# A recurrent-attention kernel gets a table of PE places, late values spread over the steps, 32-column values, one softmax product per unit and a held store queue

## The chip, the cores and the metric

The kernel runs on one core of one Trainium2 chip. The metric is device time in microseconds (us) of one launch. "Before" is timed by the median of five runs: 1677.59 us (1676.94 to 1679.9). The profile is one further execution, taken by the hardware profiler. Engine names: PE is TensorE's matmul, PEld its weight load, DVE VectorE, ACT ScalarE, POOL GpSimd, SP SyncE, which here only issues DMAs.

## What is computed

Two layers, each a memory-augmented recurrent attention (A) and a dense relu layer (B), both with a layer norm in front and a residual; x is 2048 x 512 in bf16. The weights are the same in both layers.

```python
def A(x, mem0, Wq, Wk, Wv, Wo):          # M = 8 memory rows, 64 segments of 32 rows, 32 heads of 128
    mem = mem0
    for s in range(n_seg):
        h = concat([mem, x[:, 32*s:32*(s+1)]])            # 40 rows
        q, k, v = h @ Wq, h @ Wk, h @ Wv                  # per head
        scores = q @ k.T * Dh ** (-0.5)                   # masked: causal, memory rows see all
        o = softmax(scores) @ v @ Wo
        mem = o[:, :M]                                    # the next segment's memory
        outs.append(o[:, M:])
x = x + A(layernorm(x), ...)
x = x + relu(layernorm(x) @ w1) @ w2
x = x + A(layernorm(x), ...)
x = x + relu(layernorm(x) @ w1) @ w2
```

A segment needs the memory rows of the one before: within a layer the segments run in a chain.

## The kernel before

**Steps.** A step k handles segment k of layer 0 and segment k - 4 of layer 1 (`DELTA = 4`) side by side. There are 68 steps: 0 to 3 have layer 0 alone (40 columns in the attention matmuls), 4 to 63 both (80 columns), 64 to 67 layer 1 alone. In a step:

- `values` (L772): h times Wv in four parts of 8 matmuls of 512 columns. Each matmul's stationary operand is 64 columns wide, so two run side by side in 64-column tiles of the array. The result is copied from the PSUM bank (`fill`) to `vw`. `place_values` moves layer 0's rows of it into `V0` by DMA (L809).
- The 32 heads go in five `UNITS`: three of eight heads (0 to 2), two of four (3 and 4). For each unit `queries_keys` (L819; matmul L832) computes q and k of four heads in 16 matmuls each, copied from PSUM by ACT or DVE (`copy_on`, L724 on ACT, L726 on DVE). `scores` (L844) multiplies them (L861), and the softmax follows on DVE and ACT: `block` (mask, L872), `top` (L876), `sub` (L879), `exp` on ACT (L883), `total` (L886), `recip` (L889), `mul` (L909). The product P is transposed on PE (`turn`, by `across`, L519), copied to `PT` (`keep`), and multiplied with V in `attend` (L947), whose result is copied to `OT`.
- `project` (L974) multiplies OT with Wo, all units into one bank `st`. Its result goes two ways: by DVE into `HT` of the next step (L990, the memory rows, the recurrence), and by `rows` into `OX`. Both read the one bank.

After every second step `finish_pair` transposes OX back (`turn`), adds the residual and runs `dense_layer` and `layernorm` for the 64 rows of each layer.

**Late values.** Layer 0's own rows are known from the start. For the first 16 of each segment's 32 rows the values are computed ahead, 16 groups of four segments (`late_values`, L752, four parts each), and stored in DRAM (`vh`). `place_values` fetches them into `V0` (L802) for each step. Groups 1 to 4 (`EARLY`) use w1's and w2's room before these weights are loaded; later ones use `vg`.

**Order.** Nothing is left to a scheduler at build time: a class `Plan` collects operations with an engine, an assumed cost, what they read and write and a buffer, orders all of them and emits them in that order, so that each engine's queue is fixed. In before it schedules forward and backward three times (`PASSES`), with one assumed latency per engine (`LAT`), one priority offset per kind of operation (`AHEAD`), and four numbers (`RULE`: how far ahead it looks, what staying in a tile mode is worth, and when an operation marked `spare` is put off or fills a gap). `spare` are the late values. Operations of tile `EITHER` run in whole tiles or in 64-column tiles, whichever PE is in. `copy_op` and the products may go to either of two engines, by whichever ends first.

**Weights.** `load_weights` (L381) issues eight DMAs of 2 MB on POOL in the order v0, v2, q0, k0, q2, k2, o0, o2. The plan assumes a landing time for each (`available`); the stores of `vh` and the loads on SP are ordered after an assumed time `loaded`, but wait for nothing. `prepare` (L461) sets buffers to zero on DVE or POOL.

The softmax product of a large unit goes in two halves, each on POOL or DVE; of a small one in one:

```python
        for b0, b1 in ((0, 1), (1, 2)) if nx == 2 else ((0, 2),):
...
            plan.op((POOL, DVE), (t_pool(2 * na * L), t_dve(2 * na * L)), mul, r=[es, sm],
                    w=[("P", p, b, x) for b in range(b0, b1) for x in xs])
```

Of the kernel before, what the change touches and what calls it, by code (L numbers as in the profile page):

```python
# [20 lines left out]

PE, ACT, DVE, POOL, SP = range(5)
LAT = (0.26, 0.16, 0.16, 0.20, 1.70)

WHOLE, COL64, EITHER = range(3)
TURN = 0.11
PASSES = 3

RULE = (0.052, 0.937, 39.167, 24.322)
AHEAD = {
    "attend.ev": -1.96, "attend.mm": -0.95, "dense_layer.mm": -0.85, "dense_layer.relu": 5.2, "finish_pair.add": -5.1,
    "finish_pair.add0": 0.5, "finish_pair.add1": -6.36, "finish_pair.turn": 2.26, "finish_pair.widen": 0.01,
    "late_values.cp": -9.2, "late_values.put": 0.92, "layernorm.aggr": -7.15, "layernorm.keep": 0.04,
    "layernorm.norm": -2.92, "layernorm.power": -0.26, "layernorm.stats": 2.48, "layernorm.turn": -30.25,
    "load_dense.dma1": -1.13, "load_dense.dma2": -2.4, "load_group.get": -0.77, "load_weights.dma": -0.55,
    "make_ident": 4.63, "make_mask": 7, "place_values.dma": 17.27, "prep_x.cp": -1.81, "prepare.get_memory": -2.96,
    "prepare.get_x": -8.86, "prepare.keep": -0.84, "prepare.place": 0.28, "prepare.zero": -0.64,
    "prepare.zero_banks": -5.82, "prepare.zero_columns": -5.11, "prepare_group.load": -0.14,  # L40
    "prepare_group.put": -0.18, "project.ev": 10.38, "project.first": 0.18, "project.mm": -0.98,
    "project.rows": -4.33, "queries_keys.ev": 4.81, "queries_keys.mm": 0.09, "scores.block": 0.96,
    "scores.exp": -1.91, "scores.keep": -25.3, "scores.mm": 0.21, "scores.mul": -8.63, "scores.recip": -1.72,
    "scores.sub": -9.57, "scores.top": 1.48, "scores.total": 48.55, "scores.turn": 1.1, "values.mm*": -36.32,
}

LOAD, BESIDE = 5.5, 0.4

EARLY = 4


def t_act(n):
    return 0.09 + 0.833e-3 * n


def t_dve(n, rate=1):
    return 0.085 + 1.042e-3 * n / rate
# [5 lines left out]

class Pool:


    def __init__(self, tiles, ordered=False):
        self.tiles, self.ordered, self.asked = tiles, ordered, 0

    def reset(self):  # L70
        self.free, self.taken = [(0.0, i, None) for i in range(len(self.tiles))], 0
# [7 lines left out]
    def when(self, bufs):  # L79
        if len(self.free) < len(bufs) or self.ordered and bufs[0].no != self.taken:  # L80
            return 1e9
        return sorted(f[:2] for f in self.free)[len(bufs) - 1][0]

    def take(self, b):
        f = min(self.free, key=lambda f: f[:2])
        self.free.remove(f)
        self.taken += 1
        b.i = f[1]
        return f[2]
# [12 lines left out]
class Op:  # L102
    __slots__ = ("eng", "cost", "fn", "preds", "succs", "bufs", "new", "given", "ready", "start", "end", "wait",
                 "after", "seq", "tile", "lag", "mode", "more", "both", "spare")


class Plan:
    def __init__(self):
        self.ops, self.writer, self.readers = [], {}, {}
        self.given = {}  # L110
# [4 lines left out]
    def op(self, eng, cost, fn, r=(), w=(), tile=WHOLE, lag=None, more=0.0, spare=False):  # L115
        o = Op()
        o.both = dict(zip(eng, cost)) if isinstance(eng, tuple) else None
        if o.both:
            eng, cost = eng[0], cost[0]
        o.eng, o.cost, o.fn, o.succs, o.seq, o.tile = eng, cost, fn, [], len(self.ops), tile  # L120
        o.mode, o.more, o.spare = tile, more, spare
        o.lag = LAT[eng] if lag is None else lag
# [26 lines left out]
    def forward(self, prio):  # L149

        look, stay, far, room = RULE
        for pool in self.pools:
            pool.reset()
        for b in self.bufs:
            b.left, b.end = len(b.users), 0.0  # L160
        for o in self.ops:
            o.wait, o.ready, o.after = len(o.preds), o.given, []
        free = [0.0] * 5
        cand = [[] for _ in range(5)]
        for o in self.ops:
            if not o.wait:
                for e in o.both or (o.eng,):
                    cand[e].append(o)
        count, tile = 0, WHOLE
        while count < len(self.ops):  # L170
            best = None
            for e in range(5):
                lo, starts = None, []
                for o in cand[e]:
                    t = max(o.ready, free[e])
                    if o.both and any(max(o.ready, free[i]) + c < t + o.both[e] for i, c in o.both.items() if i != e):
                        continue
                    for pool, bufs in o.new:
                        t = max(t, pool.when(bufs))
                    starts.append((t, o))  # L180
                    if lo is None or t < lo:
                        lo = t
                if lo is not None and lo < 1e9 and (best is None or lo < best[0]):
                    best = (lo, e, starts)
            assert best is not None, "no operation can be planned"
            lo, e, starts = best
            def rank(c):
                return (prio[c[1].seq] - (stay if e == PE and c[1].tile in (tile, EITHER) else 0.0), c[1].seq)

            t, o = min((c for c in starts if c[0] <= lo + look), key=rank)  # L190
            if e == PE and o.spare:

                soon = [c for c in starts if t < c[0] < t + o.cost and prio[c[1].seq] < prio[o.seq] - far]
                if soon:
                    due = min(c[0] for c in soon)
                    t, o = min((c for c in starts if c[0] + room * c[1].cost * c[1].spare <= due and c[0] <= due), key=rank)
            o.start = t
            for i in o.both or ():
                if i != e:
                    cand[i].remove(o)  # L200
            if o.both:
                o.eng, o.cost, o.lag = e, o.both[e], LAT[e]
            cand[e].remove(o)
            for pool, bufs in o.new:
                for b in bufs:
                    last = pool.take(b)
                    if last is not None:
                        o.after += last.users
            o.end = o.start + o.cost
            if e == PE:  # L210
                o.mode = tile if o.tile == EITHER else o.tile
                if o.mode != tile:
                    o.end, tile = o.end + TURN, o.tile
                if o.mode == COL64:
                    o.end += o.more
# [869 lines left out]
```

## Time and profile before

| what | value |
|---|---|
| median of five runs | 1677.59 us |
| the profiled execution | 1679.95 us, span 1678.2 us |
| mean granted TensorE clock | 0.994 |
| matmuls of queries and keys (L832) | 17,408: 15,360 of 80 columns, 2,048 of 40 |
| matmuls of the projection (L974) | 8,704: 7,680 of 80 columns, 1,024 of 40 |
| value matmuls in 64-column tiles (L780) | 2,688: 2,176 of the steps, 512 late ones |
| softmax products (L909) | 270 on DVE, 274 on POOL |
| HBM traffic | 33.89 MB read, 12.45 MB written |

The span is the time from the first to the last instruction; launch and end lie around it. Busy time of PE holds pipelined matmuls whose ends are modelled: the mean of a matmul's row (200 ns for L832) is its time in the pipe, not its pace. The pace is read from the starts of successive groups in the timeline. In a row "work<-HT,Wq_sb" is out<-in by the kernel's tile names; a wait is written as the waiting row, then "<-" and what released it.

### The profile page before, as it was taken

What the parts mean: (1) busy time and instruction counts of PE and PEld (TensorE: products, weight loads), DVE (VectorE), ACT (ScalarE), POOL (GpSimd) and SP (SyncE); (2) the same over time, 40 slices, a digit from 0 to 9 for tenths busy, and PEclk for the clock granted to TensorE, in tenths of its full rate; (3) what the DMA queues carried; (4) which work ended last, traced back from release to release, by engine and by line L of the source; (5) the groups of instructions that cost most, each with busy time, mean ns of one, the idle gap of its engine ahead of it and who ended that gap; (6) DMA issues with size and microseconds to landing.
All of it is one profiled execution on the core that took longest, in us unless ns stands there. A gap on an engine that the chain in (4) does not pass through costs nothing.

```text
span 1678.2 us, 90465 instructions
## 1 busy us (share of the span) xinstructions
PE 1627.0 (97%) x40568; PEld 1395.8 (83%) x40568; DVE 1066.5 (64%) x3090; ACT 1062.7 (63%) x2679; POOL 246.1 (15%) x603
## 2 busy tenths in 40 slices
PE   6899999999999999999999999999999999999998
PEld 3678888888888888888888888888888888888886
DVE  5457566666676575667666665676566656766655
ACT  3466666666666666666666666666666666666664
POOL 3111111111111111111111111111111111111100
PEclk9899999999999999999999999999999999999999
DMA  9711111111110101000000000101010000000000
GB/s 369 238 49 35 38 38 27 35 41 33 32 39 18 37 18 31 22 21 24 19 24 21 20 22 18 27 18 25 19 27 16 19 23 21 18 18 19 18 5 7
DMA packets 32503, 64.88 MB, mean 39 GB/s; under 512 B 7049, under 2 KB 16913, under 8 KB 32113
## 3 DMA queue, kind: packets, MB, share of 16 engines
q1 hardware_dynamic: 25984, 39.38, 8.6%
q0 software_dynamic: 4608, 18.19, 2.9%
q8 instruction: 318, 5.21, 1.3%
q10 hardware_dynamic: 1520, 1.52, 0.3%
q14 instruction: 73, 0.59, 0.1%
HBM read 33.89 MB, written 12.45 MB: 28 GB/s over the span
## 4 chain that ended last, share of the span: by engine, by line
PE 79%; DVE 13%; DMA 4%; issue 1%; ACT 1%; POOL 1%; SPq 0%; POOLq 0%; DVEq 0%; ACTq 0%
PE work L832 32%; PE fill L780 16%; PE st L974 13%; PE fill L519 8%; PE work L947 3%; PE work L861 3%; DMA Wo_sb<-in_A_Wo_dram 3%; PE work L519 2%; DVE OT L726 2%; DVE sm L886 2%; DMA V<-vw 2%; DVE PT L726 1%; DVE ln L528 1%; DVE xg L616 1%; POOL P L909 1%
## 5 line engine op out<-in xcount | busy, mean ns | idle before, releaser
L832 PE MATMUL work<-HT,Wq_sb 128*128 128x80 bf16 (+1 forms) x8704 | 391.0, 200 | 7.5 <-DVE HT L990 6.7
L832 PE MATMUL work<-HT,Wk_sb 128*128 128x80 bf16 (+1 forms) x8704 | 390.2, 199 | 6.9 <-DMA Wk_sb<-in_A_Wk_dram 4.5
L974 PE MATMUL st<-OT,Wo_sb 128*128 128x80 bf16 (+1 forms) x8704 | 354.3, 200 | 2.5 <-DMA Wo_sb<-in_A_Wo_dram 2.3
L832 PEld LDWEIGHTS <-Wq_sb 128*128 128x128 bf16 x8704 | 333.0, 99 | 26.7 <-issue 9.5
L832 PEld LDWEIGHTS <-Wk_sb 128*128 128x128 bf16 x8704 | 336.5, 100 | 8.5 <-DMA Wk_sb<-in_A_Wk_dram 5.4
L974 PEld LDWEIGHTS <-Wo_sb 128*128 128x128 bf16 x8704 | 322.3, 100 | 23.1 <-issue 17.8
L872 DVE TENSOR_TENSOR es<-work,maskb 128x320 f32<-128x320 f32 (+2 forms) x340 | 137.4, 404 | 304.7 <-PE work L861 291.3
L909 POOL TENSOR_TENSOR P<-es,sm 128x160 bf16<-128x160 f32 (+1 forms) x274 | 127.4, 466 | 1214.3 <-ACT kT L724 485.7
L780 PE MATMUL fill<-Wv_sb,HT 128*64 128x512 bf16 x2176 | 281.5, 383 | 0.0
L724 ACT CAST qT<-work 128x320 bf16<-128x320 f32 (+1 forms) x500 | 204.9, 410 | 82.1 <-PE work L832 62.0
L724 ACT CAST kT<-work 128x320 bf16<-128x320 f32 (+1 forms) x489 | 200.2, 409 | 76.1 <-PE work L832 31.8
L724 ACT CAST PT<-work 64x320 bf16<-64x320 f32 (+2 forms) x451 | 163.0, 363 | 112.4 <-PE work L519 69.5
L724 ACT CAST vw<-fill 128x512 bf16<-128x512 f32 x221 | 129.5, 586 | 101.1 <-PE fill L780 92.6
L724 ACT CAST OT<-work 128x320 bf16<-128x320 f32 (+1 forms) x374 | 145.3, 410 | 60.1 <-PE work L947 58.2
L780 PEld LDWEIGHTS <-HT 128*64 128x64 bf16 x2176 | 102.0, 110 | 62.7 <-issue 1.8
L883 ACT ACTIVATE es<-es 128x320 f32<-128x320 f32 (+2 forms) x340 | 135.0, 404 | 23.2 <-DVE es L879 14.1
L886 DVE TENSOR_REDUCE sm<-es 128x8 f32<-128x320 f32 (+2 forms) x340 | 133.5, 399 | 25.4 <-ACT es L883 22.7
L876 DVE TENSOR_REDUCE mx<-es 128x8 f32<-128x320 f32 (+2 forms) x340 | 135.1, 398 | 3.2
L879 DVE TENSOR_TENSOR es<-es,mx 128x320 f32<-128x320 f32 (+2 forms) x340 | 134.3, 401 | 1.6
L861 PEld LDWEIGHTS <-qT 128*40 128x40 bf16 x4096 | 91.4, 98 | 43.4
L726 DVE CAST PT<-work 64x160 bf16<-64x160 f32 (+2 forms) x229 | 87.5, 382 | 61.0 <-ACT PT L724 48.0
L947 PE MATMUL work<-PT,V 128*64 128x80 bf16 (+1 forms) x1504 | 114.6, 202 | 8.8 <-ACT PT L724 5.8
(89 smaller groups left out, 1854.4 us busy)
## 6 DMA issues: line engine op xcount, KB each, us to landing
V<-vw SPq DMA_DIRECT2D x252, 48.0 KB
V<-vh SPq DMA_DIRECT2D x126, 64.0 KB
vh<-vg SPq DMA_DIRECT2D x12, 512.0 KB
Wv_sb<-in_A_Wv_dram POOLq DMA_DIRECT2D x2, 2048.0 KB, 11.1
Wq_sb<-in_A_Wq_dram POOLq DMA_DIRECT2D x2, 2048.0 KB, 22.4
Wk_sb<-in_A_Wk_dram POOLq DMA_DIRECT2D x2, 2048.0 KB, 29.2
Wo_sb<-in_A_Wo_dram POOLq DMA_DIRECT2D x2, 2048.0 KB, 42.1
vh<-w_sb SPq DMA_DIRECT2D x4, 512.0 KB
```

The source lines that it names most:

```text
L519: nc.tensor.matmul(out_[u:v, :], lhsT=lhsT[:, u:v], rhs=rhs, start=start, stop=stop, tile_position=(0, u))
L724: nc.scalar.copy(out=out_, in_=in_)
L726: nc.vector.tensor_copy(out=out_, in_=in_)
L780: nc.tensor.matmul(vp[64 * b:64 * b + 64, :], lhsT=cols[:, c4, :], rhs=Wv_sb[:, c4, n * 512:(n + 1) * 512], start=(c4 == 0), stop=(c4 == N ...
L832: nc.tensor.matmul(qp[:, hi * 2 * L:hi * 2 * L + n], lhsT=W_sb[:, c4, h * Dh:(h + 1) * Dh], rhs=HT[:, c4, c0:c1], start=(c4 == 0), stop=(c ...
L861: nc.tensor.matmul(v[64 * g2:64 * g2 + L, a, b, i, :], lhsT=qT[:, hi, a * L:(a + 1) * L], rhs=kT[:, hi, a * L:(a + 1) * L], start=True, st ...
L872: nc.vector.tensor_tensor(out=flat(es[:, A]), in0=flat(sp[:, A]), op=ALU.add, in1=maskb[:, a_lo:a_hi, :].unsqueeze(2).to_broadcast([128, n ...
L876: nc.vector.tensor_reduce(out=mx[:, As], in_=es3(), axis=AX.X, op=ALU.max)
L886: nc.vector.tensor_reduce(out=sm[:, As], in_=es3(), axis=AX.X, op=ALU.add)
L909: (nc.gpsimd if eng == POOL else nc.vector).tensor_tensor(out=o, in0=e, in1=sv.unsqueeze(3).to_broadcast([128, na, 2, L]), op=ALU.mult)
L947: nc.tensor.matmul(o[u:u + cols, :, a, :], lhsT=V[:, p, e0 + u:e0 + u + cols], rhs=PT[:, a, 2 * i + h2, :, :], start=True, stop=True, tile ...
L974: nc.tensor.matmul(wo[:, 2 * W * c4 + c0:2 * W * c4 + c1], lhsT=Wo_sb[:, h, c4 * 128:(c4 + 1) * 128], rhs=OT[:, h, c0:c1], start=(h == 0 a ...
```

## The change

1. **Places.** A table `PLACE` gives a priority for each PE operation of a step by its kind, unit, number and the step's parity; a step counts `PERIOD`. The planner goes forward once instead of three times forward and backward. Other operations take their priority from their consumers. `LAT` is a latency for each pair of engines, PSUM banks are held from one engine to the next, and the assumed costs are others.
2. **Late values.** Part p of group g (from 5 on) is given the step 4g - 8 + p; before, they had no step. Their store goes in two halves.
3. **Narrow values.** In steps 0 to 3 `values_narrow` replaces `values`: 32 columns instead of 64 as the stationary operand, four 32-column tiles side by side, two banks instead of four.
4. **One product.** The softmax of a unit ends in one `mul` over all its heads, on POOL or DVE; the scores are laid out so that it is one access pattern.
5. **Weights.** v goes as 1 + 1 + 2 MB. A small DMA on SP (`hold`) reads the last rows of Wo and is the producer of `loaded`: SP's stores and loads that read `loaded` come behind it.
6. `turn` takes its PT buffer at the transpose instead of at the copy.

```diff
+RULE = (0.0474, 165.9433, 849.1155, 931199.0135)
+PERIOD = 35.7447
+PLACE = {
+    ("attend.mmu0.0", 0): -216.486, ("attend.mmu0.0", 1): 347.606, ("attend.mmu1.0", 0): 191.045,
...
+    ("finish_pair.turn.0", 1): -571.909, ("g0", 0): 141.998, ("g1", 0): 105.737,
...
+    def rank_ops(self):
+        for o in reversed(self.ops):
+            if PE in o.cost:
+                o.prio = PERIOD * o.step + PLACE.get((o.key, o.step % 2), 0.0)
+            else:
+                e, c = min(o.cost.items(), key=lambda x: x[1])
+                o.prio = min((s.prio - (LAT[e][min(s.cost)] if o.lag is None else o.lag) for s in o.succs),
+                             default=PERIOD * (o.step + 3)) - c - AHEAD.get(o.kind, 0.0)
...
-        for i, part in enumerate(("v0", "v2", "q0", "k0", "q2", "k2", "o0", "o2")):
+        for c, p0, n in (("v", 0, 1), ("v", 1, 1), ("v", 2, 2), *((c, p0, 2) for cc, p0 in (("qk", 0), ("qk", 2), ("o", 0), ("o", 2)) for c in cc)):
...
+        def hold():
+            nc.sync.dma_start(out=held[:], in_=Wo_sb[0:1, H - 1, 0:16])
+
+        plan.op(SP, 0.78, hold, r=[("W", "o", 2)], w=["loaded"], lag=0.0)
...
-        values(XG[:, :, :], room, name, ["XG"])
+        values(XG[:, :, :], room, name, ["XG"], 4 * g - LEAD if g > EARLY else None)
+        for p0, p1 in ((0, 4),) if g <= EARLY else ((0, 2), (2, 4)):
+            def put(p0=p0, p1=p1):
+                nc.sync.dma_start(out=vh[g][:, p0:p1, :], in_=room[:, p0:p1, :])
...
-    def values(cols, dst, name, deps):
+    def values(cols, dst, name, deps, step=None):
         for p in range(4):
+            if step is not None:
+                plan.mark(step + p, f"v{p}")
...
+    def values_narrow(cols, deps):
+        for u in range(2):
+            vp = b_fill.buf()
+            def mm(vp=vp, u=u):
+                for c4 in range(NC4):
+                    for i in range(4):
+                        n = 4 * u + i
+                        nc.tensor.matmul(vp[32 * i:32 * i + 32, :], lhsT=cols[:, c4, :],
+                                         rhs=Wv_sb[:, c4, n * 512:(n + 1) * 512],
+                                         start=(c4 == 0), stop=(c4 == NC4 - 1), tile_position=(0, 32 * i))
...
+        if 1 in act:
+            values(HTs[i][:, :, HS:2 * L], vw, ("vw",), deps)
+        else:
+            values_narrow(HTs[i][:, :, HS:HS + 32], deps)
...
-        for b0, b1 in ((0, 1), (1, 2)) if nx == 2 else ((0, 2),):
...
+        def mul(eng):
+            o = P[:, :].rearrange("p (a c) -> p a c", a=2)[:, a_lo:a_hi, 128 * xs[0]:128 * xs[-1] + 128]
+            o = o.rearrange("p a (s k) -> p a s k", k=64)[:, :, :, 0:L]
+            (nc.gpsimd if eng == POOL else nc.vector).tensor_tensor(
+                out=o, in0=flat(es[:, A]), op=ALU.mult,
+                in1=sm[:, As].rearrange("p (a s) -> p a s", a=na).unsqueeze(3).to_broadcast([128, na, ns, L]))
+        plan.op((POOL, DVE), (t_pool(n), t_dve(n)), mul, r=[es, sm], w=[("P", p, b, x) for b in range(2) for x in xs])
...
-        plan.op(PE, nx * na * 0.0365, turn, r=[*[("P", p, b, x) for b in range(2) for x in xs], "ident"], w=[tp], tile=EITHER)
         PT = p_PT.buf()
+        plan.op(PE, nx * na * 0.0358, turn, r=[*[("P", p, b, x) for b in range(2) for x in xs], "ident"], w=[tp, PT],
+                tile=EITHER)
```

## Predicting the time of the changed kernel

> **What bounds the kernel now.** I read the page's busy shares first, then the 40 slices, the busy time by stretch, PE's waits in the first and in a late stretch, and last the timeline for the pace of a matmul.
>
> ```profile
> span 1678.2 us, 90465 instructions
> PE 1627.0 (97%) x40568; PEld 1395.8 (83%) x40568; DVE 1066.5 (64%) x3090; ACT 1062.7 (63%) x2679; POOL 246.1 (15%) x603
> PE   6899999999999999999999999999999999999998
> PEclk9899999999999999999999999999999999999999
> DMA  9711111111110101000000000101010000000000
> ```
>
> PE is the bound at full clock; the other engines idle a third of the time or more. Only the first two slices (84 us) show PE below nine tenths, and there the DMA engines are the busy ones.
>
> ```profile
> 0.00:100.00 100.00, 75.78 (x1617) 54.13 (x1617) 50.42 (x178) 46.25 (x129) 24.17 (x70) 0.93 0.72 260
> 100.00:560.00 460.00, 458.11 (x11164) 389.04 (x11165) 301.94 (x841) 298.42 (x741) 74.52 (x186) 1.00 0.12 35
> 1040.00:1600.00 560.00, 551.98 (x13999) 483.24 (x13996) 361.25 (x1030) 364.02 (x901) 74.66 (x173) 1.00 0.08 20
> ```
>
> The columns are stretch, length, then busy us of PE, PEld, DVE, ACT, POOL, clock, DMA share, GB/s. Idle PE: 24.2 us at the start, 1.9 in the next 460, 8.0 in a late 560. A busy PE is not yet at its pace, so I take the pace from starts in the timeline:
>
> ```profile
> 905.40 1.05 PE L780 MATMUL fill<-Wv_sb,HT 128*64 128x512 bf16 x8
> 907.50 1.03 PE L780 MATMUL fill<-Wv_sb,HT 128*64 128x512 bf16 x8
> 908.36 0.31 PE L519 MATMUL work<-ident,P 128*64 128x80 bf16 x8
> 909.19 0.74 PE L832 MATMUL work<-HT,Wk_sb 128*128 128x80 bf16 x16
> 909.76 0.74 PE L832 MATMUL work<-HT,Wq_sb 128*128 128x80 bf16 x16
> ```
>
> 16 matmuls of 80 columns take 0.57 (36 ns each); 8 of 512 columns in 64-column tiles 907.50 to 908.36 (0.86, 108 ns each, half of what a full tile's 512 columns take). 40 columns go at 25 ns, from starts 0.40 apart at 62 us. All 40,568 matmuls laid end to end at such paces: 1530.8 us. The 495 changes between whole and 64-column tiles cost 0.096 into and 0.117 to 0.204 out of them (medians of start-to-start gaps): some 56. Before the first matmul lie 3.7, after the last start 4.2. 1678.2 minus these leaves 83.7 us of waits, by start-to-start gaps 29.6 in the first 100 us, 6.5 to 560, 38.2 from 560 to 1600, 9.4 after. The change can win only there and in the 1587.
>
> PE's waits from 560 to 1600 (total, times, longest), then those of the first 100 us:
>
> ```profile
> PE work L832 <- DVE HT L990: 6.4, 20, 0.3
> PE work L947 <- ACT PT L724: 5.5, 21, 0.3
> PE work L947 <- DMA V<-vw: 1.7, 4, 0.5
> ```
>
> ```profile
> PE fill L519 <- DVE xr L540: 6.1, 2, 5.5
> PE work L832 <- DMA Wk_sb<-in_A_Wk_dram: 4.5, 2, 3.7
> PE work L832 <- issue: 2.4, 1, 2.4
> PE st L974 <- DMA Wo_sb<-in_A_Wo_dram: 2.3, 2, 1.4
> ```
>
> Late, the same two waits recur once in two steps: the next step's first matmuls for HT, the last unit's attend for PT. They show about a third of the 38.2; gaps around transposes, too short to be listed, hold the rest. They cost 1.7 us in two steps after 560 us and 0.3 to 0.4 before, where late values (independent matmuls) stand in the gaps. At the start PE waits for weights.
>
> **1. 32-column values, steps 0 to 3.** Each step's 32 matmuls in 64-column tiles become 32 in 32-column tiles. Before shows no such tile. Bounds: four side by side, by the halving from full tile to 64, 54 ns; no gain, 108. Four steps: 128 × (108 − 54) = 6.9 us saved, or 0. I take 6.9, continuing the step the trace has. Two evictions a step replace four, on engines that idle here.
> The Trainium skill (TensorE: Matmul & The Clock Gate, "Measured speedup vs the span model") speaks against full scaling: three 32-column tiles gave 2.38×, 79% of three. The trace's pair shows its full 2×. By the page's share the saving would be an estimated 5.1.
>
> **2. The order of PE.** Built, it has 532 tile changes against 495: 37 × 0.113 = +4.2 (3.5 to 7.5, by the dear exits at 0.204). Parts 1 and 2: −2.7.
>
> **3. Late values one part a step.** 44 parts leave the early steps and stand two in each odd step up to step 43; before they were used up by 560 us (step 18). Matmuls unchanged. I compare, in the new order, the PE work between producer and consumer with what the chain needs. HT needs 0.49 (DVE copy 225 ns and hops); the order allows 1.31 to 1.51 up to step 43: this wait goes. From step 44, the transposes of finish_pair follow the last project at once, and they need HT, then OX (ACT waits for DVE in the same bank), 0.95: +0.9 each odd step.
>
> **4. One softmax product per unit.** Before: halves, 234 on DVE and 246 on POOL for the large units:
>
> ```profile
> L909 DVE TENSOR_TENSOR P<-es,sm 128x160 bf16<-128x160 f32 x234 | 80.6, 353 | 3.6
> L909 POOL TENSOR_TENSOR P<-es,sm 128x160 bf16<-128x160 f32 x246 | 118.2, 482 | 1115.7 <-ACT kT L724 485.7 <-DVE sm L889 403.6 <-ACT qT L724 80.9
> ```
>
> After: DVE does 336 of 340 whole. No 320-wide product is in the trace; its neighbours (L879, the same operation on 320 columns) take 482 ns. On the chain 0.48 replaces 0.35 (DVE half) or 0.48 (POOL half): +0.13 to 0, taken as +0.1. DVE load: 180 × 0.48 + 143 × 0.32 + 13 × 0.24 = 135 against 89 before, while 50 copies of vw (691 ns) move to ACT: +11 us in all. Both engines idle a third, so the load itself is free; where the cover fails is unit 2's chain. In the new DVE order I count, from the end of its scores: hop 0.2, three dependent passes to 1.72, exp 0.47 and two hops to 2.49 (a qT/kT copy and unit 3's block lie under it), total 0.40, unit 3's top 0.27, recip 0.12, unit 3's sub 0.27, product 0.48, hop 0.13: about 4.2. The order allows 4.0 in even steps (there the next unit's passes lie under exp: needs 4.0 to 4.1), 3.95 in odd steps with late values, 3.1 in odd steps without. Units 3 and 4 queue behind: their turns another 0.2 to 0.3 late. Per two steps: 0.55 up to step 43 (20 pairs, 11 us); 1.1 + 0.9 + 0.3 = 2.3 after (10 pairs, 23). Together 34 against 6.5 + 38.2 = 44.7: −10.7. Bounds: by the pure chain of 3.9 (no queue) and all others met, 20, −25; by before's actual 4.7 for units 0 to 2 (its queue carried over), 20 × 1.3 + 10 × 3.1 = 57, +12.
>
> **5. Weights hold back stores.** SP gets one DMA that reads Wo's last rows, so everything behind it on SP waits until all weights are in.
>
> ```profile
> 13.39 44.65 DMA Wo_sb<-in_A_Wo_dram
> 71.55 7.19 DMA V<-vw
> ```
>
> These are pieces of the chain that ended last. Wo ends at 58.0. Until then 16.8 MB of weights and five vh stores (2.6 MB) share the engines, at 393 GB/s from 20 to 40 us. Without the stores: 2.6/393 = 6.7 us earlier, 51.4. Against it: memsets of three x tiles move into POOL's queue between the v loads, v comes as 1 + 1 + 2 MB, and the first transposes wait for DVE about 2.3 longer (norm near 11 instead of 8.9): values begin near 14.6 instead of 11.2. That lies before the wait for Wk (landing at 31.3) and costs nothing; uncovered it would cost the 3.4. Step 1's queries (start 61.66) come at 54 to 56. Step 1's order is 2.6 us shorter already (part 1 and earlier fill), so of the 7 some 5 count here. Next late: behind the hold SP has some ten DMAs, four 0.5 MB stores among them (5.3 us at 393), then V for step 1; by these it lands at 64 to 66, wanted near 66. I charge 2 (0 to 6). Later late puts are split into halves, 11 more issues on SP, whose queue has long gaps then: 0. Net −3 (−9 to +5).
> The skill's DMA: Bandwidth & Descriptors ("Bandwidth") gives a 1 MB transfer 78% of peak, which speaks against the split of v; no 1 MB weight load is in this trace. By the page's 6.15 us each, the two halves would take an estimated 12.3 us against the 11.1 that the page of DMA issues shows for 2 MB of Wv: 1.2 lost ahead of the wait for Wk, which covers it.
>
> **6. The tail** (steps 64 to 67, layer 1 alone): the same chains with less work between, order distances 0.1 to 0.2 shorter for unit 4: +1 (−1 to +4).
>
> **Sum.** −2.7 − 10.7 − 3 + 1 = −15.4 against the profiled 1679.95 (span 1678.2 and 1.75 around it): 1664.5. That execution stands 2.4 above the median of 1677.59, so the median goes to 1662.2.
>
> **Rivals.**
> - *Slower: DVE's softmax chain becomes the bound.* With no product on POOL, each unit's chain passes DVE alone, and the order allows units 2 to 4 only 3.1 to 4.5, against 4.6 to 5.1 before. If units really need what units 0 to 2 took before (4.7 to 5.2), turns of units 2, 3 and 4 lag: about 0.7 a step more than I charge, 60 steps × 0.7 = 42: 1704. It decides from 0.27 a step (16 us). For: 0.65 of queue in the old chains. Against: DVE idles 35%, and the old queue held vw copies that leave. 0.12.
> - *V comes late.* SP's backlog delays V of step 1 by 8 instead of 2: 1668. The 7.19 us transfer above speaks for it. 0.13.
> - *32-column tiles run two wide:* +6.9, 1669. 0.08.
> - *All steady waits vanish* (chain 3.9): 1662 − 14 = 1648. For: 0.3 per pair before 560 us. Against: finish_pair after step 44. 0.12.
> - *The change doesn't do what it says:* same shortfalls as before; only parts 1, 2, 5, 6 count: −4.7, 1673, in and out of the no-change band. 0.10.
> My forecast, 1655 to 1670: 0.45.
>
> 0.2% is 3.4 us, about what a measurement can tell from no change: 1674.2 to 1681.0. Below: 0.45 + 0.13 + 0.08 + 0.12 and 0.03 of the last: 0.81. Within: the other 0.07 of it. Above: the first rival, 0.12. Range 1648 to 1680: the low end is the rival without waits, the high end startup's and the chain's dear bounds in part.
>
> **What would show it.** L780 losing 128 matmuls, the new narrow line's starts 54 ns apart (108: part 1 wrong). PE's wait for Wo near 51, then how long step 1's attend waits for V. PE waits from 560: HT gone up to step 43; after it (last 500 us) transposes of OX and P waiting 2 to 2.5 in two steps. Wrong altogether: PE below nine tenths in the middle slices, waiting for DVE's P in every step.

## The result, and the profile after

The changed kernel takes 1674.35 us (median of 23 runs, 1671.82 to 1677.27) against 1678.4 for the kernel before in the same comparisons (41 runs, 1676.24 to 1681.14). The ratio is 0.9976, 95% interval [0.997, 0.9981]: faster by 4.05 us. The forecast was 1662. Its sign was right; of its gain of 15.4 us a quarter came.

The profiled execution took 1673.42, 6.5 less than before's. Its page begins (busy us, shares of the span; then busy tenths of 40 slices):

```profile
span 1671.7 us, 87959 instructions
...
PE 1619.3 (97%) x39689; PEld 1387.0 (83%) x39689; DVE 1049.5 (63%) x3065; ACT 1090.4 (65%) x2759; POOL 127.4 (8%) x337
...
PE   6799999999999999999999999999999999999997
...
PEclk9999999999999999999999999999999999999999
DMA  9811011111101111101110100010000000000000
```

POOL has lost all but 4 of its products, ACT has gained 28 us, nearly all copies, PE is still the bound at full clock, and the first two slices are still the ones where it idles. Busy time by stretch (columns as before):

```profile
0.00:100.00 100.00, 74.15 (x1798) 55.12 (x1798) 50.64 (x181) 46.65 (x138) 26.31 (x70) 0.97 0.76 264
100.00:560.00 460.00, 458.18 (x11219) 394.38 (x11216) 294.91 (x850) 312.81 (x781) 33.80 (x93) 1.00 0.11 30
560.00:1040.00 480.00, 478.94 (x11527) 411.41 (x11523) 306.31 (x860) 325.16 (x800) 33.30 (x91) 1.00 0.10 27
1040.00:1600.00 560.00, 545.53 (x13381) 473.32 (x13381) 360.43 (x1031) 368.40 (x916) 31.07 (x77) 1.00 0.08 20
```

From 560 to 1040 PE now idles 1.1 us (before: 7.3 by the same view), but from 1040 to 1600 14.5 (before: 8.0). PE's waits from 1100 to 1600 (total, times, longest):

```profile
PE work L516 <- DVE P L930: 7.5, 10, 0.8
PE fill L516 <- ACT OX L721: 4.6, 10, 0.5
```

The waits for HT and for the last PT, which the profile of before showed here, are gone. In their place stand the transposes of unit 2 waiting for its product, and those of `finish_pair` waiting for OX, each once in two steps. Both are waits that the prediction named for the steps from 44 on.

These views list only gaps between busy spells. To place the time I took PE's start-to-start gaps in each trace, less the paces and tile changes of the prediction. What is left is waiting, in us:

| steps | before | after | forecast of the difference | found |
|---|---|---|---|---|
| up to step 1's first query | 26.4 | 24.1 | | −2.3 |
| 1 to 3 | 8.4 | 11.5 | −3 with the line above | +3.1 |
| 4 to 43 | 25.2 | 14.9 | −10.7 with the line below | −10.3 |
| 44 to 63 | 17.3 | 23.4 | | +6.1 |
| 64 to 67 | 10.1 | 9.5 | +1 | −0.6 |
| matmuls and tile changes | 1586.7 | 1584.0 | −2.7 | −2.7 |

The sum is −6.7, against −6.5 between the two profiled executions. The start (PE; start, length, then the wait in brackets):

```profile
11.88 0.61 PE L516 MATMUL fill<-ident,xr 128*128 128x128 bf16 x4 [11.88 <-DVE xr L537]
...
54.84 2.23 PE L996 MATMUL st<-OT,Wo_sb 128*128 128x40 bf16 x64 [0.89 <-DMA Wo_sb<-in_A_Wo_dram]
...
61.14 1.05 PE L799 MATMUL fill<-Wv_sb,HT 128*32 128x512 bf16 x16
62.12 0.38 PE L889 MATMUL work<-kT,qT 128*40 128x40 bf16 x16
...
71.98 0.40 PE L860 MATMUL work<-HT,Wq_sb 128*128 128x40 bf16 x9 [4.40 <-issue]
```

The first transposes come at 11.88 (9.45 before). Wo is there at 54.8, 3.2 earlier than before, where 51.4 was forecast. 16 value matmuls in 32-column tiles take 0.98 from start to start: with a tile change in it, 54 to 55 ns each, as forecast. Then, in the middle of one group of 16 matmuls of step 1, PE stands for 4.4 us and the trace shows nothing that it waits for. Up to then SP has issued what the held queue let go (54.8 to 68.2, almost without a pause), and the DMA engines are full (a share of 1.03 from 65 to 70). Before had such a gap too, of 2.4.

### The profile page after: what moved, and what is told of

The parts are those of the page before. It is cut to its first block, busy times and chain, and to the rows that moved or that the text cites. A ratio compares the mean times of both kernels' runs of the same rounds, so it can differ in the third digit from the quotient of the medians.

```text
span 1671.7 us, 87959 instructions
## 1 busy us (share of the span) xinstructions
PE 1619.3 (97%) x39689; PEld 1387.0 (83%) x39689; DVE 1049.5 (63%) x3065; ACT 1090.4 (65%) x2759; POOL 127.4 (8%) x337
## 4 chain that ended last, share of the span: by engine, by line
PE 83%; DVE 6%; ACT 5%; issue 3%; DMA 2%; POOL 0%; POOLq 0%; DVEq 0%; ACTq 0%
PE work L860 32%; PE st L996 18%; PE fill L780 15%; PE fill L516 10%; PE work L969 3%; PE work L516 3%; PE work L889 2%; ACT PT L721 2%; DMA Wo_sb<-in_A_Wo_dram 2%; DVE P L930 1%; DVE sm L914 1%; DVE es L907 1%; ACT es L911 1%; DVE mx L904 1%; ACT qT L721 1%
## 5 line engine op out<-in xcount | busy, mean ns | idle before, releaser
L860 PE MATMUL work<-HT,Wk_sb 128*128 128x80 bf16 (+1 forms) x8704 | 357.4, 199 | 1.5 <-issue 0.8
L860 PE MATMUL work<-HT,Wq_sb 128*128 128x80 bf16 (+1 forms) x8704 | 345.6, 199 | 4.4 <-issue 4.4
L860 PEld LDWEIGHTS <-Wk_sb 128*128 128x128 bf16 x8704 | 322.2, 99 | 28.8 <-issue 17.0
L860 PEld LDWEIGHTS <-Wq_sb 128*128 128x128 bf16 x8704 | 317.4, 99 | 6.8 <-issue 4.5
L780 PE MATMUL fill<-Wv_sb,HT 128*64 128x512 bf16 x2048 | 261.3, 382 | 0.0
L721 ACT CAST OT<-work 128x320 bf16<-128x320 f32 (+1 forms) x400 | 157.5, 421 | 118.8 <-PE work L969 114.8
L721 ACT CAST vw<-fill 128x512 bf16<-128x512 f32 x263 | 153.3, 583 | 95.4 <-PE fill L780 87.6
L911 ACT ACTIVATE es<-es 128x320 f32<-128x320 f32 (+2 forms) x340 | 138.3, 409 | 24.1 <-DVE es L907 23.0
L1012 DVE CAST HT<-st 128x64 bf16<-128x64 f32 (+1 forms) x67 | 14.8, 221 | 208.1 <-ACT OX L721 208.1
L930 DVE TENSOR_TENSOR P<-es,sm 128x320 bf16<-128x320 f32 (+2 forms) x336 | 141.7, 424 | 5.2
L969 PE MATMUL work<-PT,V 128*128 128x80 bf16 (+1 forms) x1188 | 109.1, 202 | 1.5 <-ACT PT L721 0.5
## 6 DMA issues: line engine op xcount, KB each, us to landing
Wv_sb<-in_A_Wv_dram POOLq DMA_DIRECT2D x1, 2048.0 KB, 11.1
```

What stands on the lines that cost most here:

```text
L721: nc.scalar.copy(out=out_, in_=in_)
L780: nc.tensor.matmul(vp[64 * b:64 * b + 64, :], lhsT=cols[:, c4, :], rhs=Wv_sb[:, c4, n * 512:(n + 1) * 512], start=(c4 == 0), stop=(c4 == N ...
L860: nc.tensor.matmul(qp[:, hi * 2 * L:hi * 2 * L + n], lhsT=W_sb[:, c4, h * Dh:(h + 1) * Dh], rhs=HT[:, c4, c0:c1], start=(c4 == 0), stop=(c ...
L911: nc.scalar.activation(out=es[:, A], in_=es[:, A], func=ACTF.Exp, scale=SCALE)
L930: (nc.gpsimd if eng == POOL else nc.vector).tensor_tensor(out=o, in0=flat(es[:, A]), op=ALU.mult, in1=sm[:, As].rearrange("p (a s) -> p a ...
L969: nc.tensor.matmul(o[u:u + cols, :, a, :], lhsT=V[:, p, e0 + u:e0 + u + cols], rhs=PT[:, a, 2 * i + h2, :, :], start=True, stop=True, tile ...
```

## The experiments

The ratio is to the kernel before, run beside each; 0.001 is 1.7 us. "After" is the changed kernel, 0.9976. But for the late values, the odd steps from 5 to 63 have nearly the same order, so an edit of one step's order acts 30 times. By the profiles, steps 4 to 63 take 1469.0 us in after and 1468.9 to 1469.8 in the runs that leave these steps alone (1, 4 and 6). The start repeats less well: step 4 starts between 115.7 and 118.3 in the eight profiled executions whose first steps are those of after (after and runs 7, 8, 9, 11 to 14).

### Parts undone, and parts alone

**1. No hold** (`a_nohold`): the small DMA is left out, its place in the order stays.

```diff
-            nc.sync.dma_start(out=held[:], in_=Wo_sb[0:1, H - 1, 0:16])
+            pass
```

> The changed kernel without the DMA that SP waits for; the order of every queue stays, so the vh stores go out as soon as their data is there. Theory (the hold gives back in step 1 what it wins before it): Wo lands 3 to 6 us later than 54.8, but PE's gap of 4.4 us in the middle of step 1's queries (for which no engine is named, while SP's backlog keeps the DMA engines full) shrinks to 2 or less; the total is within 2 us of the changed kernel (ratio to before 0.9965 to 0.999). Rival (the hold is worth what its 2.6 MB cost at 393 GB/s): 4 to 7 us slower than the changed kernel, ratio 1.000 or above.

Measured: 1674.85, ratio 0.9982 [0.9974, 0.9991], not told apart from after. By its profile Wo lands at 56.7, 1.9 later than in after (not 3 to 6), step 1's queries start at 59.7 instead of 57.6, steps 1 to 3 wait 11.1 instead of 11.5, and step 4 starts at 118.9 against 117.3. So the hold brings Wo 1.9 forward, and in these two executions most of that is still there at step 4; the medians, 0.5 apart, can't tell it from nothing. The gap of PE did not shrink to 2 or less: it is 2.71 here, and a second one of 1.23 follows. So the gap is not the hold's doing.

**2. The product in halves again, in the new order** (`a_split`): one half on POOL, one on DVE, at the place of the one product.

```diff
+            for i in range(nx):
...
+                (nc.gpsimd if i == 0 and nx == 2 else nc.vector).tensor_tensor(
```

> The changed kernel with the product of a large unit as two instructions at the same place of the order, one half on POOL and one on DVE; all else stays. Theory (the whole product on DVE is what makes unit 2's transposes late by 0.2 us in every step and by 0.9 in odd steps from 44): the chain gets 0.1 to 0.15 shorter on DVE but the POOL half (482 ns) ends about with the whole one, so the waits of scores.turn 2 shrink by at most 0.1 a step: 0 to 6 us faster. Rival (the order alone sets those waits, the product's form is indifferent): within 1 us. If POOL's half comes later than the whole product did, slower by up to 6.

Measured: 1680.24, ratio 1.0013 [1.0004, 1.0022]. The single product is worth 6 us in the new order. With halves the steps 4 to 63 wait 43.3, as much as before's 42.5: with halves, the new order and the spread values bring nothing in waits, and cost their 4.2 of tile changes. (The order was drawn up for one product; an order made for halves was not tried.)

**3. The single product in the old order** (`b_one`): the kernel before, with one product on DVE at the place of the second half.

```diff
+            def mul(eng, b1=b1):
+                if b1 < 2:
+                    return
```

> The kernel before with one softmax product per unit on DVE, at the place of its second half; the order of all else stays, and POOL has no product. Theory (the single product is what the change gains, since the changed kernel with halves again took 6 us more): 3 to 7 us faster than before (ratio 0.996 to 0.998). Rival (the single product pays only in the new order, which gave DVE the room by moving vw copies to ACT): the same or up to 8 us slower.

Measured: 1689.09, ratio 1.0067 [1.0053, 1.0081]: 11 us slower. The single product, worth −6 in the new order, costs +11 in the old one. PE's waits from 560 to 1600 in that run are led by

```profile
PE work L519 <- DVE P L905: 14.9, 23, 0.7
```

which is the mechanism of the prediction's slower rival. It exists; the new order, which also moved most copies of `vw` from DVE to ACT, leaves enough room for it.

**4 and 5. The price of the narrow values.** `a_twice`: after, each 32-column value matmul done twice into the same bank. `b_narrow`: before, its order kept, with 32-column values in steps 0 to 3.

```diff
-                for c4 in range(NC4):
+                for c4 in 2 * list(range(NC4)):
```

> The changed kernel with every 32-column value matmul of steps 0 to 3 done twice into the same bank with the same result: 128 matmuls more. It prices the narrow values alone. Theory (four tiles run side by side, 54 ns each, and in steps 1 to 3 PE has nothing else to wait for): +5.2 if step 0's 32 lie under the wait for weights, +6.9 if not, so 1679.5 to 1681.3, and the waits of steps 4 to 67 unchanged. Rival (the start is set by the weights and the value rows, narrow values only shift where PE waits): 0 to +2, 1674.4 to 1676.4.

> The kernel before, its order unchanged, with 32-column values in steps 0 to 3 (two of the four value operations of a step do nothing, the two others run four 32-column tiles; V's rows go by four small transfers instead of two). Theory: the narrow values bring what they save in matmul time in any order, -5 to -7: 1671.5 to 1673.5, so this part alone is as good as the whole change. Rival (steps 1 to 3 of before wait for weights and V anyway): -2 to 0, 1676.5 to 1678.5.

Measured: 1680.09, ratio 1.0014 [1.0005, 1.0023], and 1678.29, ratio 1.0006 [0.9997, 1.0015]. In after the 128 added matmuls cost 5.7 by the medians; step 4 starts 5.9 later, of which 0.75 is there at step 1's queries (step 0's 1.7 lie mostly under the wait for Wo) and 5.2 in steps 1 to 3. So the narrow values are worth some 6 there. In the kernel before they are worth nothing that the comparison shows. By its profile steps 1 to 3 are 2.9 shorter, not 5.2. Why the median shows none of these 2.9 stays open: V's rows go by more transfers there, Wo came 0.54 later in that execution, and the two profiled executions are far from their medians (this one 1.6 below, before's 1.55 above), so that the 2.9 itself may be the spread of single executions.

**6. Early first transposes** (`a_early`): the bank memsets behind the first norms, the identity made early.

> The changed kernel with DVE's 2.65 us of bank memsets behind the first three norms and POOL's identity matrix right behind the first weight load: the first transposes come at 9.5 instead of 11.9. Theory (what comes before Wo has landed is covered: Wo at 54.8 sets step 1): within 1 us of the changed kernel. Rival (the late first transposes cost their 2.4 us): 2 to 3 us faster.

Measured: 1673.8, ratio 0.9974 [0.9964, 0.9984], as after. The transposes start at 9.25 instead of 11.88 and step 0's queries 3.0 earlier (1.8 in run 15); all of it is lost again at the weights. This lateness was costed at nothing, rightly.

### Moving work within a step

What holds unit 2's product in odd steps? The timeline of step 51 in after, whose first query starts at 1270.53 (DVE, ACT, then PE):

```profile
1283.89 0.49 DVE L907 TENSOR_TENSOR es<-es,mx 128x320 f32<-128x320 f32 x1
...
1285.29 0.49 DVE L914 TENSOR_REDUCE sm<-es 128x8 f32<-128x320 f32 x1 [0.26 <-ACT es L911]
...
1286.28 0.49 DVE L930 TENSOR_TENSOR P<-es,sm 128x320 bf16<-128x320 f32 x1
```

```profile
1283.91 0.85 ACT L721 CAST PT<-work 64x320 bf16<-64x320 f32 x2
1284.79 0.47 ACT L911 ACTIVATE es<-es 128x320 f32<-128x320 f32 x1
```

```profile
1286.82 0.34 PE L516 MATMUL work<-ident,P 128*64 128x80 bf16 x8 [0.79 <-DVE P L930]
```

Unit 2's subtraction ends at 1284.38. Its exponential could follow at once, but ACT is copying unit 0's PT until 1284.76. The transposes start 16.29 after the step's first query, the order would allow 15.4. From unit 1's first pass to unit 2's product DVE has no gap over 0.12 but for the 0.26 shown. Overall both engines are busy two thirds of the time; in this half of the step they are full.

**7. One values part behind unit 2's scores** (`a_part3`), to lengthen the PE work under the chain in odd steps.

```diff
+            mm.start = at[(k, "scores.mmu2.0")].start + 0.001
+            ev.start = mm.start + 1.2
```

> The changed kernel with part 3 of the step's values moved, in odd steps 5 to 63, from before the scores of unit 1 to behind those of unit 2, and its DMA to V split from that of part 2. This puts 0.87 us of PE work between unit 2's scores and its transposes. Theory (unit 2's softmax chain needs about 4.2 us and the order gives 3.1 in steps without late values): the wait of unit 2's transposes falls from 0.93 to near 0.1 in odd steps from 44 and from 0.22 to 0 in odd steps before: 9 + 4 = 13 us at most, less what attend 3 waits for V (0 to 0.4 in 30 steps): 3 to 12 us faster than the changed kernel. Rival (the transposes wait for a DVE queue that is full, so that later work behind it moves along): under 2 us faster, the wait moving to units 3 and 4 or to finish_pair.

Measured: 1686.81, ratio 1.0055 [1.0042, 1.0067]. The wait did not shrink (0.96 from step 44 on, and 0.5 instead of 0.23 before it): the part's own copy went into ACT's queue ahead of the exponential, which starts 0.44 later in the step although DVE's subtraction is done 0.85 earlier.

**8. The exponential ahead of unit 0's second PT copy** (`a_exp2`).

```diff
+            at[(k, "scores.expu2.0")].start = at[(k, "scores.keepu0.1")].start - 0.001
+            for o in ops:
+                if o.spare and a0.start < o.start < s4.start:
+                    o.start = a0.start - 0.001
```

> The changed kernel with, in odd steps 5 to 63, unit 2's exp on ACT ahead of the second PT copy of unit 0 instead of behind it, and a late value that stood between attend 0 and unit 4's scores put ahead of attend 0. Theory (ACT's queue, not the chain itself, makes unit 2's transposes 0.25 us late: its sub ends at 13.86 in step 51 and its exp starts at 14.26, when ACT is through with unit 0's PT copies): the wait of scores.turn 2 falls by 0.2 to 0.25 in each of 30 odd steps: 4 to 7 us faster than the changed kernel (ratio to before 0.9935 to 0.995). Rival (attend 0 then comes 0.3 later and takes the place of that wait): within 1.5 us.

Measured: 1690.85, ratio 1.0075 [1.0063, 1.0088]. From step 44 on the wait of unit 2's transposes falls from 9.25 to 4.45 in all, and unit 0's `attend`, whose copy now comes later, takes 3.4 of it; PE's waits from 1100 to 1600 show the exchange:

```profile
PE work L516 <- ACT OT L721: 2.7, 10, 0.3
PE work L969 <- ACT PT L721: 2.4, 10, 0.4
```

Up to step 43 the moved late value costs more than it saves (waits 14.9 to 29.7, with extra tile changes).

**9. POOL's cast away from unit 2's product** (`a_widen`), and **10.** runs 6, 8 and 9 together (`a_both`). In even steps the product takes 669 ns in the median, in odd ones 485; a cast on POOL (L677) runs beside it in the even ones. The cast is put later; from step 9 on it then reads rows that have been replaced, so these rows' residual comes from a later group.

```diff
+            if o.kind == "finish_pair.widen" and o.step > 8:
+                o.start = 0.001 + min(q.start for q in ops if q.key == "prep_x.cp.1" and q.start > o.start)
```

> The changed kernel with the cast of finish_pair's rows on POOL (widen, 0.71 us) moved from the middle of the even step before to behind the copy of the layer 1 rows in the odd step, where DVE has a gap of 2 us. Theory (unit 2's product takes 669 ns in even steps against 485 in odd ones because POOL's cast runs beside it, and the transposes wait 0.19 for it): the product goes to 490 and the wait to near 0 in 30 even steps: 3 to 6 us faster (ratio to before 0.994 to 0.996). Rival (the product is slow for another reason, or the wait is set by the queue behind): within 1.5 us.

> Both of these edits and the earlier first transposes together. If the three act in different places, the gains add: 7 to 13 us faster than the changed kernel, 1661 to 1667. If they share a wait: no more than the larger one.

Measured: 1674.77, ratio 0.9974 [0.9963, 0.9985], and 1691.3, ratio 1.0078 [1.0065, 1.009]. The product falls to 492 ns in even steps too and unit 2's wait there from 5.9 to about 0.7 over all even steps; unit 4's transposes (3.5) and the `attend` of units 2 and 3 take it over, and the sum of waits stays as it was. The second run adds nothing to run 8.

### Taking load away, and a swap

After runs 7 to 10 two readings were left: any order hands the wait on to the next unit, or ACT's queue ahead of the exponential has to be relieved without burdening another queue.

**11 and 12. Lighter queues, same order** (`a_lact`, `a_lboth`).

```diff
+                if p == 0 and 8 <= k < NSEG:
+                    a_to, to = 1, ns * L
+                copy_on(eng, PT[R, a_lo:a_to, 0:2 * nx, b, :],
```

> The changed kernel, its order unchanged; in steps 8 to 63 the two ACT copies of unit 0's transposed P move a half of their columns (layer 0 alone), so that layer 1's attention of that unit reads old values. It takes load from ACT's queue ahead of unit 2's exponential and moves nothing. Theory (a full ACT queue stands ahead of that exponential in odd steps 44 to 63): the wait of unit 2's transposes there falls from 0.93 to about 0.6, no other wait grows by as much, -3 to -6 in all: 1668.5 to 1671.5. Rival (the waits come from the chain's own length, or the next unit takes them over as when operations were moved): within 1.5 of the changed kernel, 1673 to 1676.

> As the run with lighter ACT copies, and also DVE's maximum and subtraction of unit 3 in steps 8 to 63 over layer 0 alone (half of the columns, so that layer 1's softmax of that unit goes without its maximum): DVE runs them between the steps of unit 2's chain. Theory (both queues are full in the second half of a step): the wait of unit 2's transposes falls further, to 0.3 to 0.45 in odd steps 44 to 63, and those of units 3 and 4 with it; -7 to -12 in all: 1662.5 to 1667.5. Rival (chain length or hand-over to the next unit): within 3 of the changed kernel.

Measured: 1666.51, ratio 0.9935 [0.9921, 0.9949], and 1663.47, ratio 0.9916 [0.9903, 0.993]: 7.8 and 10.9 below after. Step 51 of the first, from a first query at 1264.02 (ACT, PE, then DVE):

```profile
1277.40 0.58 ACT L721 CAST PT<-work 64x160 bf16<-64x160 f32 x2
1278.01 0.47 ACT L911 ACTIVATE es<-es 128x320 f32<-128x320 f32 x1
...
1278.93 1.09 ACT L721 CAST OT<-work 128x320 bf16<-128x320 f32 x3
```

```profile
1280.04 0.33 PE L516 MATMUL work<-ident,P 128*64 128x80 bf16 x8 [0.68 <-ACT OT L721]
```

```profile
1279.50 0.48 DVE L930 TENSOR_TENSOR P<-es,sm 128x320 bf16<-128x320 f32 x1
```

The two copies take 0.58 instead of 0.85, the exponential starts 0.27 earlier in the step, the transposes 0.27 earlier (16.02). By the two profiles steps 4 to 63 are 7.15 shorter: 0.26 in each odd step from 45 on, 0.18 in each of the 20 before them, where the transposes start 0.24 earlier and other waits take over a part, and 0.03 in an even step. What releases the transposes now is ACT's last copy of OT (to 1280.02), 0.04 behind the product (to 1279.98). So what these copies cost is load in ACT's queue, ahead of the exponential and of the copies behind it, and not the length of DVE's chain alone. My expectation put it too low (−3 to −6), since it counted the steps from 44 on alone. In the second run the transposes start at 15.86.

**13. A swap, with all work done** (`a_swap`): unit 0's second PT copy goes to DVE, and one q/k copy of unit 4 from DVE to ACT, behind the exponential.

```diff
+                keep.eng, ev[0].eng = DVE, ACT
+                keep.start, ev[0].start = block.start - 0.001, exp.start + 0.001
```

> The changed kernel; in odd steps 5 to 63 the second copy of unit 0's transposed P goes from ACT to DVE and the copy of unit 4's second q/k tile from DVE to ACT, behind unit 2's exponential. No work is added or left out, each engine has the same number of copies. Theory (ACT's queue ahead of unit 2's exponential sets these waits): the exponential starts 0.27 earlier as in the run with lighter ACT copies, 30 odd steps x 0.25 = -7.5: 1665.5 to 1668.5. Rival (load is only handed on, unit 4's scores or unit 0's attend take the wait over): within 2 of the changed kernel, 1672 to 1676.

Measured: 1670.9, ratio 0.9955 [0.9942, 0.9967]: faster than both kernels, 3.45 below after. Step 51, first query at 1269.32:

```profile
1283.27 0.47 ACT L911 ACTIVATE es<-es 128x320 f32<-128x320 f32 x1
```

```profile
1283.21 0.49 DVE L723 CAST PT<-work 64x320 bf16<-64x320 f32 x1
1283.73 0.33 DVE L900 TENSOR_TENSOR es<-work,maskb 128x160 f32<-128x160 f32 x1
1283.97 0.48 DVE L914 TENSOR_REDUCE sm<-es 128x8 f32<-128x320 f32 x1
```

```profile
1285.49 0.34 PE L516 MATMUL work<-ident,P 128*64 128x80 bf16 x8 [0.74 <-DVE P L930]
```

The exponential starts at 13.95 after the first query instead of 14.26, 0.31 earlier. But DVE's copy waits for the subtraction, the next unit's mask pass waits for the copy, and the sum behind it starts at 14.65, where 14.49 was possible with lighter copies. Of 0.27 a step 0.12 is kept: 30 × 0.12 = 3.6, against 3.45 by the medians and 3.0 by steps 4 to 63 of the profiles. The truth lies between the two readings.

**14 and 15.** The swap with unit 3's subtraction behind unit 2's product (`a_swap_sub`), and the swap with early first transposes (`a_swap_early`).

```diff
+            if sub.start < mul.start:
+                sub.start = mul.start + 0.001
```

> As a_swap, and DVE's subtraction of unit 3 goes behind unit 2's product in these steps. Theory (DVE's interleaved passes lengthen unit 2's chain): 30 x 0.1 less for unit 2's transposes, unit 3 has room in most steps: -1 to -3 against a_swap. Rival (unit 3's exponential, late by 0.4, holds ACT's copies and unit 3's transposes): 0 to +6 against a_swap.

> As a_swap, with the bank memsets behind the first norms and the identity made early (as in the run with early first transposes). Theory (that wait is covered by the one for the weights): within 1 of a_swap. Rival: -2.

Measured: 1676.12, ratio 0.9991 [0.9982, 1.0], and 1670.74, ratio 0.9959 [0.9945, 0.9972]. The first is 5 above the swap: unit 2's `attend` now waits 7.8 over the odd steps up to 43, and unit 3's transposes 2.1 after them. The late exponential of unit 3 stands ahead of unit 2's PT copies on ACT. The second repeats run 6: no difference.

## Why the prediction was right or wrong, point by point

**Bound and view of it.** Right: PE set the time, and only its waits and its own matmuls could be won. What the prediction drew from "both engines idle a third" was wrong: that is a mean over the step, and in the half of the step where the softmax chains lie the queues have no room (runs 7 to 12). DVE's load, forecast 11 us up, fell by 17: the single product added 51, but beside the copies of `vw` (35) some of OT and PT (24) went to ACT.

**1 and 2, narrow values and order, −2.7: right in size** (1586.7 to 1584.0). Four 32-column tiles run four wide; the 37 tile changes are paid. Run 4 prices the first in after at some 6. The rule weighed here, from the Trainium skill (TensorE: Matmul & The Clock Gate, "Measured speedup vs the span model"), gives three 32-column tiles 2.38×; this case's four gave 108 to 54 ns against the pair of 64-column tiles, the full step.

**3 and 4, the waits of steps 4 to 63, −10.7: this is the step that failed; −4.2 came.** By parts:

- Steps 44 to 63 were "1.1 + 0.9 + 0.3 = 2.3 after (10 pairs, 23)". Found: 23.4. The sum is right in part by luck: unit 2's transposes wait 0.93 instead of 1.1, `finish_pair` 0.62 instead of 0.9, and all the rest 0.8 instead of 0.3. For `finish_pair` the chain was another one than counted. The count has HT copied first and OX behind it; so it is in before (end of step 39, DVE, then ACT; then a row of after's page):

```profile
1016.83 0.23 DVE L990 CAST HT<-st 128x64 bf16<-128x64 f32 x1 [0.72 <-PE st L974]
```

```profile
1017.09 0.37 ACT L724 CAST OX<-st 128x256 bf16<-128x256 f32 x1 [1.24 <-DVE HT L990]
```

```profile
L1012 DVE CAST HT<-st 128x64 bf16<-128x64 f32 (+1 forms) x67 | 14.8, 221 | 208.1 <-ACT OX L721 208.1
```

In the changed kernel ACT's copy to OX comes first in all 67 steps, and DVE's to HT starts 0.40 after it. OX is ready sooner; HT is later, and the views list one wait of PE for it (0.58, at 57.65).
- Steps 4 to 43 were "0.55 per two steps up to step 43 (20 pairs, 11 us)". Found: 14.9, 0.75 a pair. The term that was too small is that of even steps, counted as just met ("needs 4.0 to 4.1", allowed 4.0): the product, taken at 0.48, takes 0.669 there beside POOL's cast, and unit 2's transposes wait 0.20 (run 9). A second one lies behind it: with the product at 0.49, the chains of the units behind wait as long. For the odd steps 0.25 was counted (4.2 against 3.95) and 0.23 found, with another content: "exp 0.47 and two hops" has 0.30 of hops, and in step 51 the exponential waits 0.41 for unit 0's PT copies on ACT, which the count leaves out. Run 11 shows that these cost 0.18 to 0.26 in each odd step.
- The base was 44.7, counted from 100 us on; steps 4 to 63 alone waited 42.5. That is 2.2 of the miss.
- I had put the gain on the order as much as on the product. Runs 2 and 3 show that neither brings a gain alone: with halves in the new order, all the rest of the change included, the ratio to before is 1.0013, with the product in the old order 1.0067. The gain exists only for both. The slower rival's mechanism was real and was averted by the order.

**5, the weights, −3: this step failed too, +0.8.** Wo came at 54.8 instead of 51.4. The mis-sized term is "Without the stores: 2.6/393 = 6.7 us earlier": with the hold left out and all else kept (run 1) Wo lands at 56.7, so the hold brings 1.9. Wo's own issue went from 11.68 and 13.39 to 23.06 and 24.89, behind copies in POOL's queue, and the loads ran at 340 GB/s from 25 to 35 us; what this cost was not tried apart. Of the 4.0 by which step 1's queries came earlier, 3.1 was lost again in steps 1 to 3, where I had charged 2 for V. PE's gaps with nothing shown that it waits for are that large: 5.65 in these steps (4.40, 0.76 and 0.49), against 2.38 before; the prediction lists that gap of before and gives it no term. The hold doesn't make them; run 1 has 2.71, 1.23 and 0.75. What they are tied to stands in the last section. All this is read from one execution each, and the start spreads by 2.6. That the late first transposes cost nothing held (runs 6 and 15). The two 1 MB loads of Wv landed 5.8 and 7.1 after their issue, 6.5 by the page of DMA issues; the Trainium skill (DMA: Bandwidth & Descriptors, "Bandwidth") has 6.15.

**6, the tail, +1:** −0.6.

**The sum.** 6.5 (steady) + 3.8 (start) − 1.6 (tail) is 8.7 of the 12.1 by which the forecast was low. The rest is the step from one execution to the median: I took off 2.4, since before's profiled run stood that much above five runs. It stands 1.55 above 41, and after's stands 0.93 below its own median.

**The rivals.** "All steady waits vanish" and "32-column tiles run two wide" are ruled out by the table. "V comes late" had the place right, but the loss was in the gaps of PE; in steps 1 to 3 its profile shows no wait for V. "The change doesn't do what it says", at 1673, came nearest in time, for another reason: the waits did move, and were partly handed on.

## What to carry to other kernels

Judge the room of an engine that feeds the bound in the stretch where its chain lies, not by its share of the span, and count what stands in each queue ahead of every step of the chain, on every engine. Before moving an operation, ask who waits for the one that it overtakes: here four moves only exchanged waits, and the one that paid took a copy out of the queue ahead of the exponential and put another behind it. Where an engine stands with nothing named, count its instructions up to the gap in several runs: a fixed count points at the instructions themselves. Price parts together as well as alone; one edit was worth −6 in one order and +11 in the other.

## What the runs showed of the hardware that was not expected

- A DVE product over 320 columns, both operands in SBUF, took 485 ns alone and 669 ns beside a cast on POOL; with the cast elsewhere it was 492 (run 9). The Trainium skill (SBUF — State Buffer, "Who interferes with whom") has the later of two such operations wait until the first is done. In step 52 the product started 0.26 after the cast, which had 0.35 left by the profile, and took 0.2 longer: the direction is the rule's, the size is less.

```profile
1308.75 0.61 POOL L677 CAST xg<-xb 64x512 f32<-64x512 bf16 x1
```

```profile
1309.01 0.69 DVE L930 TENSOR_TENSOR P<-es,sm 128x320 bf16<-128x320 f32 x1
```

- PE stood still for 4.40 us inside a group of matmuls with nothing shown that it waited for, in before for 2.38, in run 4 for 2.29 (before, then run 4):

```profile
74.06 0.23 PE L832 MATMUL work<-HT,Wk_sb 128*128 128x40 bf16 x3 [2.38 <-issue]
```

```profile
70.30 0.53 PE L860 MATMUL work<-HT,Wk_sb 128*128 128x40 bf16 x15 [2.29 <-issue]
```

The traces show that the place is fixed in PE's stream of instructions and not in the work: in 16 of the 17 this gap comes after 1985 or 1986 matmuls and weight loads, whatever stands there (in after a matmul of queries, in before and in run 4 one of keys); in run 1 it comes after 1729, 256 fewer. Each time PE goes on 1.2 to 1.7 us after a packet of 16,384 bytes has landed on the DMA queue of kind instruction, always the seventh of that queue (in run 1 the sixth); in after that packet runs from 69.37 to 70.73 and PE starts at 71.98. The page counts 310 packets in this queue, one for each 256 of PE's 79,378 matmuls and weight loads. So PE waited for its own next instructions. In after the DMA engines were full just before (a share of 1.03 from 65 to 70); whether that delayed the packet was not tried.
- An ACT copy of 160 columns in place of 320 took 0.29 in place of 0.425 us: halving the columns took off a third.
